# A searched program order without warm-up matmuls, and the last output stores on two queues

## Chip, cores, metric

One core of a Trainium2 chip. The metric is the device time of that core in microseconds, from the first instruction to the last. All outputs are right.

## The reference

Attention with a mask made by clusters, then two large matrix products with an exact gelu between them. Cut to what matters:

```python
# q, k, v: 4 x 8 x 768 x 64   centroids: 8 x 16 x 64   (32 "heads" of 768 x 64)
q_assign = argmax(einsum('bhsd,hcd->bhsc', q_n, c_n))      # nearest of 16 centroids
k_assign = argmax(einsum('bhsd,hcd->bhsc', k_n, c_n))
mask     = q_assign[..., :, None] == k_assign[..., None, :]
scores   = where(mask, q @ k.T / 8, -1e9)
x        = softmax(scores) @ v                             # then 3072 x 512
out      = gelu(x @ w_in) @ w_out                          # w_in 512 x 2048, w_out 2048 x 512
```

## The kernel before

The kernel does not leave the order of its instructions to a scheduler. A long string, `TABLE`, names every operation once, and `Plan.run` emits them in that order. The order on each engine and the moment at which a buffer comes free both follow from it. A word such as `evq0@DVE` puts an operation on another engine than its usual one. A word `warm256` is no work at all: a matmul on a constant tile into a spare PSUM bank, there to keep TensorE busy.

```python
TABLE = (
    "cent loadq0 loadq1 zero3 loadk1 dm loadk0 hiq0 zero2 ident ssq ones hik0 exptab root "
    "eps loq0 warm256 warm256 ... (18 in all) trq0 rnorm lok0 hiq1 loadk2 cn chi "
    "warm256 warm256 trk0 clo loq1 evk0 warm256 warm256 ctr evq0@DVE hik1 lok1@DVE cc "
    "warm256 ... (7) asnk0 asnq0 amax0 ge0 ... warm256 warm256 ohtr0 ... "
    # ... some 2,000 more words ...
    "fc2_3_P4_2_1 c122_3 stc1223 c212_3 stc2123 "
)

class Plan:
    def run(self, table):
        # ... cut ...
        for word in table:
            name, _, eng = word.partition("@")
            if name.startswith("warm"):
                self.filler(int(name[4:]))
                continue
            op = by_name[name]
            assert op not in done and done.issuperset(op.deps), name
            # ... takes its buffers, which have to be free ...
            op.emit(*([eng or op.eng] if op.alt else []))

plan = Plan(POOLS, lambda n: nc.tensor.matmul(warm_ps[:, 0:n], dm[:, 0:128],
                                              dm[:, 128:128 + n], start=True, stop=True))
```

Words that the argument needs, for head i:

- `loadq`, `loadk`, `loadv`: the head's inputs come in. `hi` casts q or k to 16 bits, `lo` subtracts to get the rest ("split"); most run on GpSimd.
- `trq`, `trk`, then `evq`, `evk`: six transposes on TensorE and the copy out of PSUM (heads 0 to 9). Later heads are transposed by a DMA (`dtr`).
- `asn`: small matmuls with 16 columns against the centroids; `amax` and `ge` turn them into a one-hot tile; `ohtr` (TensorE) or `ohd` (DMA) transposes it; `putk`, `putq` write it into the 16 spare rows of the transposed k and q. A score matmul then adds a large constant where the clusters agree.
- `sc`, `exp`, `av`, `rec`, `norm`: scores, exponentials (ScalarE), attention times V, normalisation. `fc1`, `gelu`, `fc2`: the two products, the second by a seven-product (Strassen) scheme whose sums (`S`, `t`, `ws`, `c`, `u`, `p`) VectorE, GpSimd and ScalarE share. `st`: output stores.

The one-hot write, and the store:

```python
def put_q(eng="DVE", i=i, e=e):                      # 16 x 768, SBUF to SBUF (PSUM for heads 0-7)
    src = T["ohps", i0][64 * e:64 * e + C, :]
    dst = T["qT", i][D:D + C, :]
    # ... ScalarE's form cut ...
    nc.vector.tensor_scalar(dst, src, float(VAL), None, op0=ALU.mult)

def store(name, j, t, col, due):
    st = add("SP", 0.36, due, lambda: nc.sync.dma_start(
        out=out_w[b][:, NJ * t + j, col * DB:(col + 1) * DB],
        in_=T[name, b, j]), [sums_out[name, j]], dma=0.45, name=f"st{name}{j}{b}")
```

The softmax here doesn't subtract the row's maximum and nothing guards it: scores larger than these inputs give would overflow.

## Time and profile before

| | before |
|---|---|
| time | 291.55 us median of 3 runs (291.4 to 291.79) |
| span of the profiled execution | 289.8 us |
| TensorE busy | 284.4 us, 3398 matmuls, of which 32 warm-ups |
| first score matmul in the chain | 11.27 us |
| first first-layer matmul in the chain | 44.76 us |
| last matmul ends | 286.62 us |
| last matmul to the end | 3.18 us |

The last four rows are read from the chain of work that ended last. A chain line gives start, duration, engine, tile written, source line and how many instructions stand in a row. They cut the span in four parts: the start, the middle stage (attention of the first heads), the long stretch of products mixed with later heads, and the tail. The prediction below shows these lines.

### The profile page before, as it was taken

How to read it: one execution, taken by the hardware profiler on the slowest of the kernel's cores; microseconds unless marked ns; L12 is line 12 of the kernel's file. 1: busy time of each engine (PE TensorE's matmuls, PEld its weight loads, DVE VectorE, ACT ScalarE, POOL GpSimd, SP SyncE). 2: the span in 40 equal slices, each digit the busy share in tenths (PEclk: the TensorE clock that was granted, in tenths of full speed). 3: DMA queues.
4: the chain of work that ended last, by engine and by line, in shares of the span. 5: the costliest groups of instructions: out<-in, count | busy, mean ns of one | idle time of the engine just before them, and what ended most of it. 6: DMA issues, size and time to landing. Idle time of an engine off the chain costs nothing.

```text
span 289.8 us, 8355 instructions
## 1 busy us (share of the span) xinstructions
PE 284.4 (98%) x3398; PEld 213.0 (73%) x3398; DVE 204.2 (70%) x494; ACT 235.1 (81%) x333; POOL 108.0 (37%) x148
## 2 busy tenths in 40 slices
PE   8999999999999999999999999999999999999995
PEld 6887766677677777765677878766687788756884
DVE  4989788397998778643489875725778833787863
ACT  4899988699799999977799988957699988599510
POOL 5898834609120631117202031605622271328000
PEclk9999999999999999999999999999999999999999
DMA  7999998899666799976479899753134213200023
GB/s 249 249 268 248 256 214 230 207 174 177 160 175 139 146 227 187 188 192 168 127 156 177 156 222 187 191 128 75 27 30 118 56 50 97 77 2 0 20 74 127
DMA packets 78038, 43.11 MB, mean 149 GB/s; under 512 B 55472, under 2 KB 78000, under 8 KB 78000
## 3 DMA queue, kind: packets, MB, share of 16 engines
q1 hardware_dynamic: 73488, 38.16, 57.7%
q0 software_dynamic: 4224, 4.19, 8.9%
q8 instruction: 26, 0.43, 0.6%
q10 hardware_dynamic: 288, 0.23, 0.3%
q14 instruction: 12, 0.10, 0.1%
HBM read 27.30 MB, written 6.29 MB: 116 GB/s over the span
## 4 chain that ended last, share of the span: by engine, by line
PE 96%; DVE 2%; ACT 1%; issue 0%; DVEq 0%
PE op L1233 25%; PE hp L918 22%; PE sc_ps L783 21%; PE x_ps L815 12%; PE fx_ps L1054 6%; PE asn_ps L615 2%; PE warm_ps L372 2%; PE tr_ps L573 2%; DVE kqT L714 1%; DVE kqT L723 1%; PE asn_ps L613 1%; PE asn_ps L612 1%; PE oh_ps L691 1%; ACT p_sb L792 1%; PE fin_ps L886 0%
## 5 line engine op out<-in xcount | busy, mean ns | idle before, releaser
L792 ACT ACTIVATE p_sb<-sc_ps 128x768 f16<-128x768 f32 x192 | 146.0, 810 | 9.7 <-PE sc_ps L783 6.8
L783 PE MATMUL sc_ps<-kqT 80*128 80x384 f16 x384 | 93.5, 325 | 0.6 <-DVE kqT L714 0.3
L918 PE MATMUL hp<-xt,w_in_sb 128*128 128x384 f16 x384 | 65.6, 326 | 0.0
L815 PEld LDWEIGHTS <-p_sb 128*128 128x128 f16 x1152 | 47.2, 97 | 10.4 <-DVE x_tok L842 0.6
L1233 PEld LDWEIGHTS <-g 128*128 128x128 f16 x480 | 45.3, 97 | 12.6 <-DVE g L948 0.2
L931 ACT ACTIVATE g<-hp 128x768 f16<-128x768 f32 x48 | 38.9, 810 | 19.0 <-PE hp L918 18.5
L918 PEld LDWEIGHTS <-w_in_sb 128*128 128x128 f16 x384 | 36.4, 98 | 22.9 <-issue 0.2
L815 PE MATMUL x_ps<-vaug,p_sb 128*128 128x65 f16 x1152 | 51.6, 193 | 0.0
L1233 PE MATMUL op<-w_out_sb,g 128*128 128x256 f16 x288 | 40.9, 272 | 0.0
L783 PEld LDWEIGHTS <-kqT 80*128 80x128 f16 x384 | 31.6, 98 | 4.7 <-DVE kqT L714 0.5
L1233 PE MATMUL op<-w_st,g 128*128 128x256 f16 x192 | 27.3, 272 | 0.0
L518 POOL TENSOR_TENSOR st<-k_raw,st 128x384 f16<-128x384 f32 x18 | 17.0, 943 | 24.9 <-DVE st L382 18.4
L518 POOL TENSOR_TENSOR st<-q_raw,st 128x384 f16<-128x384 f32 x21 | 19.8, 947 | 13.4 <-ACT st L380 8.6
L382 POOL CAST st<-q_raw 128x384 f16<-128x384 f32 x16 | 8.4, 531 | 40.9 <-DMA q_raw<-in_q_dram 24.9
L631 DVE TENSOR_REDUCE asb<-asn_ps 128x192 f32<-128x384 f32 x24 | 13.2, 551 | 14.8 <-PE asn_ps L615 14.6
L382 POOL CAST st<-k_raw 128x384 f16<-128x384 f32 x16 | 8.6, 537 | 35.4 <-DMA kqT<-st 16.3
L1233 PEld LDWEIGHTS <-S 128*128 128x128 f16 x192 | 18.0, 97 | 5.0
L842 DVE TENSOR_TENSOR x_tok<-x_ps,rec 128x384 f16<-128x384 f32 (+1 forms) x40 | 19.0, 476 | 1.1
L835 DVE RECIPROCAL rec<-x_ps 128x6 f32<-128x6 f32 (+1 forms) x40 | 7.4, 186 | 11.7 <-PE x_ps L815 10.7
L615 PEld LDWEIGHTS <-kqT 128*128 128x128 f16 x288 | 12.0, 96 | 3.4
L1233 PE MATMUL op<-w_st,S 128*128 128x256 f16 x96 | 13.9, 272 | 0.0
L1233 PE MATMUL op<-w_out_sb,S 128*128 128x256 f16 x96 | 13.8, 272 | 0.0
(125 smaller groups left out, 405.6 us busy)
## 6 DMA issues: line engine op xcount, KB each, us to landing
q_raw<-in_q_dram SPq DMA_DIRECT2D x32, 192.0 KB, 3.5
v_raw<-in_v_dram SPq DMA_DIRECT2D x32, 192.0 KB, 3.5
out_dram<-c SPq DMA_DIRECT2D x48, 128.0 KB, 2.0
k_raw<-in_k_dram SPq DMA_DIRECT2D x31, 192.0 KB, 3.4
w_in_sb<-in_moe_w_in_dram POOLq DMA_DIRECT2D x4, 512.0 KB, 10.4
w_out_sb<-in_moe_w_out_dram POOLq DMA_DIRECT2D x4, 512.0 KB, 8.6
kqT<-st SPq DMA_TRANSPOSE x22, 4.3
k_raw<-in_k_dram ACTq DMA_DIRECT2D x1, 192.0 KB, 3.2
```

The source lines that it names most:

```text
L382: engine[eng].tensor_copy(o, i)
L518: engine[eng].tensor_sub(t[:, :, D:2 * D], T[w + "raw", i], t[:, :, 0:D])
L615: nc.tensor.matmul(o, t[:, js], c_cat[:, h].rearrange("p a c -> p (a c)"), start=True, stop=True)
L631: nc.vector.tensor_reduce(out=T["asb", i], in_=T["asn", i].rearrange("p n w (a c) -> p n w c a", a=2), axis=AX.X, op=ALU.add)
L783: nc.tensor.matmul(s_ps[:, e, 0:QB], T["kT", i][0:D + C, c * 128:(c + 1) * 128], T["qT", i][0:D + C, t * QB:(t + 1) * QB], start=True, sto ...
L792: nc.scalar.activation(T["p", i, t][:, 2 * cp:2 * cp + 2, :], T["sc", i, t, cp][:, :, 0:QB], ACT_FN.Exp, bias=0.0, scale=float(scale))
L815: nc.tensor.matmul(o, T["p", i, t][:, ch, jj * 128:(jj + 1) * 128], vaugs[turn("va", i)][:, ch, 0:D + 1], start=(ch == 0), stop=(ch == N - 1))
L842: nc.vector.tensor_tensor(T["xtok", b][:, h // 2, j0:j0 + nn, h % 2 * D:(h % 2 + 1) * D], T["x", key][:, :, 0:D], T["rec", key].to_broadca ...
L918: nc.tensor.matmul(T["hp", hb, fp][:, e, 0:QB], w_in_sb[:, m, f * 128:(f + 1) * 128], T["xt", b][:, m, t * QB:(t + 1) * QB], start=(m == 0 ...
L931: nc.scalar.activation(T["g", hb][:, :, fp, :], T["hp", hb, fp][:, :, 0:QB], ACT_FN.Gelu, bias=0.0, scale=1.0)
L1054: nc.tensor.matmul(o, a[p](m), r[p](m), start=start and m == 0, stop=m == 1, skip_group_check=not start)
L1233: nc.tensor.matmul(T["op", b, key], a()[:, f, j * 128:(j + 1) * 128], w[:, f, :], start=(start and f == 0), stop=(f == NB - 1), skip_group ...
```

## The change

The intent: put the stores of the last row tile on two queues, so that one does not wait for the issue of the other; and take a new order from a search on a model that charges VectorE for the one-hot writes' drains and assumes that the clock rises later. That search left out all 32 warm-ups.

```diff
-    "cent loadq0 loadq1 zero3 loadk1 dm loadk0 hiq0 zero2 ident ssq ones hik0 exptab root "
-    "eps loq0 warm256 warm256 warm256 ... trq0 rnorm lok0 hiq1 loadk2 cn chi warm256 warm256 trk0 ...
+    "cent loadq1 ones dm zero3 loadk0 exptab ssq loadq0 zero2 root eps rnorm cn hik0 hiq0
+     lok0 chi clo loq0 loadk1 ident trk0 evk0 ctr trq0 hik1 cc lok1 hiq1 evq0@DVE ...
 ... (the 2,037 remaining words stand in a new order; the tail of it:)
-    "... c122_3 stc1223 c212_3 stc2123 "
+    "... stc2213 fc2_3_P3_2_0 c222_3@DVE stc2113 stc2223@ACT fc2_3_P3_2_1 c122_3
+     fc2_3_P4_2_0 fc2_3_P4_2_1 c212_3 stc2123 stc1213 stc1223@ACT "
 ...
-            st = add("SP", 0.36, due, lambda: nc.sync.dma_start(
+            st = add("SP", 0.36, due, lambda eng: engine[eng].dma_start(
                 out=out_w[b][:, NJ * t + j, col * DB:(col + 1) * DB],
-                in_=T[name, b, j]), [sums_out[name, j]], dma=0.45, name=f"st{name}{j}{b}")
+                in_=T[name, b, j]), [sums_out[name, j]], dma=0.45, name=f"st{name}{j}{b}",
+                alt={"SP": 0.36, "ACT": 0.36} if b == B - 1 and j == 2 else {"SP": 0.36})
```

By engine, the new order also moves ten two-input operations, net, from VectorE to GpSimd (245 to 235 on VectorE, 73 to 83 on GpSimd). Eight of them are subtractions of q or k (`lo`, 128x384).

## The prediction

> **What bounds the kernel now.** I read the busy table first, then the stretches by engine, then the chain that ended last, once for the first 46 us and once for the last 24 us.
>
> The page's busy and slice parts:
>
> ```profile
> PE 284.4 (98%) x3398; PEld 213.0 (73%) x3398; DVE 204.2 (70%) x494; ACT 235.1 (81%) x333; POOL 108.0 (37%) x148
> ...
> DMA  7999998899666799976479899753134213200023
> ```
>
> TensorE is counted busy for 98% of the span. That number alone would also be written by an engine that waits, because the matmuls overlap (a pair of score matmuls shows 0.49 us in the timeline and is 0.33 us apart in the chain). So I count the work from the chain instead. It gives these paces: 8 first-layer matmuls in 1.30 us (0.1625 each), 4 score matmuls in 0.65 (0.1625), 18 attention-times-V in 0.55 (0.0306), 156 second-layer in 17.04 (0.109), 96 of the last batch's first layer in 15.74 (0.164), small assignment matmuls about 0.025, transposes 0.34 per six (0.057). With the counts of the program: 384 x 0.1625 = 62.4; 384 x 0.1625 = 62.4; 1152 x 0.0306 = 35.2; 672 x 0.109 = 73.4; 112 x 0.164 = 18.4; 480 x 0.025 = 12.0; 182 x 0.057 = 10.3. Sum 274.1 us of useful TensorE work, the same in both kernels.
>
> The chain in order of time, of the early and the late part:
>
> ```profile
> 1.36 4.02 PE warm_ps L372 x18
> 5.38 0.64 PE tr_ps L573 x6
> ...
> 7.02 0.22 PE warm_ps L372 x2
> ...
> 7.35 0.77 PE warm_ps L372 x7
> 8.70 0.74 PE trs_ps L573 x12
> ...
> 11.27 0.38 PE sc_ps L783 x2
> ...
> 44.76 1.30 PE hp L918 x8
> ```
>
> ```profile
> 269.58 17.04 PE op L1233 x156
> 286.62 0.02 issue
> 286.65 0.42 DVE c L1279
> ```
>
> TensorE's part of the run goes from 1.36 to 286.62, 285.3 us. Less 274.1, 11.2 us are not useful work. Warm-up matmuls on constants take 4.02 + 0.43 + 0.22 + 0.77 + 0.22 + 0.12 = 5.8 of them. About 0.5 is the first two groups of transposes at a slower pace (0.64 and 0.58 for six, later 0.34). 4.9 us remain as gaps. Up to the first score matmul (11.27) the useful work is 3.35 us. Between the first score and the first first-layer matmul (11.27 to 44.76, 33.5 us) it is 34.04 - 3.35 = 30.7, so 2.8 us of gaps lie there. From 44.76 to 286.62 (241.9 us) there is 239.9 of work, so gaps of under 2.
>
> The stretches show what else is full in the middle stage:
>
> ```profile
> core 0: us, PE busy (x) PEld busy (x) DVE busy (x) ACT busy (x) POOL busy (x), PEclk, DMA share, GB/s
> ...
> 15.00:20.00 5.00, 5.00 (x104) 4.20 (x101) 4.31 (x12) 4.79 (x8) 4.82 (x8) 1.00 1.12 271
> 20.00:25.00 5.00, 4.80 (x98) 3.89 (x95) 4.57 (x12) 4.65 (x8) 4.99 (x9) 1.00 1.18 261
> ...
> 35.00:40.00 5.00, 4.63 (x81) 3.51 (x80) 4.29 (x11) 4.33 (x7) 1.71 (x4) 1.00 1.07 191
> ```
>
> VectorE is at 4.3 to 4.6 of 5 us, ScalarE at 4.3 to 4.8, and the DMA engines are at their full share. No single engine is the bound from 15 to 45 us; four are nearly full together. After 50 us TensorE alone is.
>
> **What the Trainium skill says.** (1) "Trainium Kernel Development and Optimization", section "Performance Expectations", calls matmul busy time a bad metric because matmuls are pipelined; the trace agrees (98% busy, 11 us without useful work), which is why I used the chain. (2) "TensorE: Matmul & The Clock Gate", Part 1, says that the array starts at half clock and goes to full clock after some 3.4 us of sustained activity, in a window that runs freely. The trace agrees: the first 18 warm-up matmuls take 4.02/18 = 223 ns each, those at 7.02 take 110 ns. The change of pace falls between 6.45 and 7.02, some 5.5 us after the first matmul. The PEclk row is 1.00 throughout and doesn't show it; only the pace does. (3) The same page, Part 4, says that transposes do not count as busy in the same way for this gate. No stretch of the trace here is only transposes, so the trace can't say. (4) "Trainium Kernel Development and Optimization", "Key Constraints": DMAs issued from several engines share the same 16 DMA engines, and issuing from several only saves the sequencer's issue time. Here an output store takes 332 ns to issue and 1.7 to 2.2 us to land.
>
> **The change part by part.**
>
> Warm-ups: all 32 are gone from the new order, 18 ahead of the first transpose, 13 before the first score, one right before it. None stands between useful work after 11.3 us, so their removal frees at most what lies on the prefix chain: 0.22 (before the one-hot transpose), 0.12, and up to 0.25 of the 0.77 group, which ended after the evacuation it covered for. About 0.5 us gained, if nothing else changed.
>
> But they also raised the clock. The new kernel's first matmul waits for a transpose's input, about 5.5 us. I walk the new prefix with durations from the old timeline. Both kernels issue the same four loads, but the new one puts head 1's q ahead of head 0's, and splits k first, which landed at 4.37. Cast 0.51, subtract 0.56: 5.5. Six transposes at half clock 0.64: 6.2. VectorE does the centroid cast (0.82), a subtract (0.23) and the q subtract (0.56) first, so the evacuation starts at 7.0; the old one started at 7.06. q's transposes end at about 7.75, and the assignment matmuls of head 0 start at 7.8 (old: about 8.1). If TensorE is still cold they take 1.2 us instead of 0.57, the twelve transposes of head 1 1.28 instead of 0.74, the one-hot transposes 0.64 instead of 0.45, six more 0.64 instead of 0.44, and head 1's assignments 1.2 instead of 0.57: 2.2 us more in all. With the old spacing (5.5 us from activity to full clock) the clock would rise at about 11, so most of this is paid, less the 0.5 gained and the 0.3 of the earlier start. I put the first score 1.2 us later (0.5 to 2), at about 12.5, and 0.6 us more lost on cold scores after it (0 to 2).
>
> Middle stage: the useful TensorE work up to the first-layer start is 34.4 instead of 34.0, ScalarE has 40 exponentials instead of 39. What moves is off VectorE: two subtractions fewer there, three more on GpSimd, one evacuation to ScalarE. VectorE's work falls from about 29.2 to 28.2 us (counts times durations of this trace: one-hot writes 0.55 + gap, evacuations 0.47, subtractions 0.46). And the new order spreads the four one-hot writes that now stand in one row (19.63 to 21.95), behind which a transpose waits. The search saw these drains, so I expect it to take 1.7 of the 2.8 us of gaps. GpSimd gets 16 subtractions of 0.945, 12 casts and 8 V casts: about 25.6 us plus some 5 of weight DMA issue, of 33. That fits, barely.
>
> Later: the same TensorE work, some other order. Of the 1.9 us of gaps I give it 0.9.
>
> Tail: two stores of the last row tile go to ScalarE's queue. In the old order SyncE's last issues are at 285.86, 286.29 and 287.10; the last follows VectorE's last add (286.65 + 0.42), so nothing was queued in front of it and a second queue has nothing to save. Worse, in the new SyncE order a store of row tile 1, whose data is ready long before, stands behind the very last one. It is issued 0.33 us later and should end the run: +0.3.
>
> Sum: +1.2 + 0.6 - 1.7 - 0.9 + 0.3 = -0.5 us, so 291.0.
>
> **Rivals.** *The clock rises as early as before* (the activity of transposes and assignments from 5.5 us is enough, and the window falls well): then the prefix costs nothing, the first score comes at 10.9 or so, and the sum is about 288.5 to 289. For it: the pieces stand close from 7 us on. Against it: gaps between 6.2 and 7.1, and matmuls of 16 columns that leave the array mostly idle. *The clock rises only when the scores flow* (transposes don't count): cold until 16 to 18 us, everything in between at half pace, 2 us more than in my sum: 293 to 295. For it: the skill's Part 4. Against: nothing in this trace. *The new DMA order becomes the wait*: the new order issues 26 head loads and all eight weight loads before the first layer instead of 22 and seven, 4 x 0.19 + 0.5 = 1.3 MB more at some 250 GB/s, 5 us of a DMA stage that is already full. Where these stand ahead of a load that is needed at once, it costs 1 to 3 us; where they are only early, nothing. *A gain of over 2%* would need 5.8 us: all gaps (4.9) and no cold loss. The floor is 5.5 + 274.1 + 3.2 = 282.8 in the trace, and the stage with four full engines makes it out of reach.
>
> **Range and chances.** The terms are small and of both signs; the cold clock (+0 to +4 together) is the widest, the middle stage (0 to -2.4) the next. A range of 288.3 to 294.3 us should hold it eight times in ten. Over 2% faster (below 285.7) 0.03, over 2% slower (above 297.4) 0.04, the rest within.
>
> **What would show it.** The first score matmul later than 11.27 by about 1 us, with transposes at 107 ns each up to 10 us or later, confirms the cold prefix; at 57 ns it refutes it. From the first score to the first first-layer matmul less than 33 us confirms the middle stage. The last SyncE issue should be a store that waits for nothing but its turn, 0.33 us after the one before; a span that ends as soon after the last matmul as before (3.2 us) refutes that. It is all wrong if GpSimd or a head load holds up the transposes between 12 and 45 us.

## The result

| | median | range |
|---|---|---|
| before (4 runs) | 291.67 us | 291.4 to 291.98 |
| after (4 runs) | 292.83 us | 292.39 to 293.24 |

The ratio is 1.0039, with a 95% interval of 1.0021 to 1.0057. Here and below a ratio is the mean time of one kernel's runs over the mean of the other's runs in the same rounds, so it is not quite the ratio of the medians quoted. The change made the kernel 0.4% slower: within 2%, inside the predicted range, but on the other side of zero from the predicted -0.5 us. Busy time of the kernel after:

```profile
PE 279.7 (96%) x3366; PEld 209.7 (72%) x3366; DVE 202.6 (70%) x483; ACT 237.5 (82%) x331; POOL 120.8 (42%) x161
```

TensorE lost its 32 warm-ups and is busy 4.7 us less, yet the span is 1.3 us longer. GpSimd is busy 12.8 us more. The chain of the kernel after, early and late part:

```profile
6.01 0.82 PE tr_ps L569 x6
...
8.83 1.25 PE trs_ps L569 x12
...
10.54 0.44 PE tr_ps L569 x6
11.57 0.48 PE sc_ps L779 x2
...
44.40 1.35 PE hp L914 x8
...
270.33 17.04 PE op L1230 x156
287.38 0.02 issue
```

TensorE now stands idle until 6.01 us. The twelve transposes at 8.83 take 1.25 us, 104 ns each; the six at 10.54 take 0.44, 73 ns each, with the clock now up. The first score comes 0.30 us later than before (11.57 against 11.27), the first first-layer matmul 0.36 us earlier (44.40 against 44.76), the last matmul ends 0.76 later (287.38 against 286.62), and the span 1.3 later. The final 156 matmuls take 17.04 us in both, so nothing is slower once the last product runs. By parts:

| part | before | after | difference |
|---|---|---|---|
| start of span to first score | 11.27 | 11.57 | +0.30 |
| first score to first layer | 33.49 | 32.83 | -0.66 |
| first layer to last matmul's end | 241.86 | 242.98 | +1.12 |
| last matmul to the end | 3.18 | 3.72 | +0.54 |
| span | 289.8 | 291.1 | +1.3 |

The new order has also moved 0.32 us more useful TensorE work ahead of the first layer (counts of matmuls by the paces given in the prediction). So in this pair of profiles the middle stage gained 1.0 us of gaps, and the long stretch, with 0.32 us less to do, lost 1.4. (Other executions of the same order lost less in the long stretch; see below the table of the experiments.) I looked for those 1.4 us by the starts of all matmuls in the two traces, taking as a gap what exceeds the normal pace by more than 0.12 us: 0.88 us in all before, 2.82 us after. The largest of the kernel after: 0.32 us at 62.8, 0.49 at 114.2, 0.42 at 116.4, 0.27 at 216.8 and 0.45 at 234.8. The wait view names the releasers; its columns are waiter, releaser, total idle us, count, longest:

```profile
PE tr_ps L569 <- DVE st L514: 6.0, 1, 6.0
...
PE sc_ps L779 <- DVE kqT L719: 0.3, 1, 0.3
PE op L1230 <- DVE p L378: 0.3, 1, 0.3
```

The second line is the stall at 234.8: a score matmul waits for a one-hot write. The timeline of the kernel after around it (start, duration, engine, line, operation, operands, count, and in brackets idle time before and its releaser):

```profile
232.63 0.42 DVE L944 TENSOR_TENSOR wf<-wf,w_in_sb 128x512 f16<-128x512 f16 x1
233.08 1.58 DVE L719 TENSOR_SCALAR kqT<-ohT 16x768 f16<-16x768 f16 x2
233.13 1.32 POOL L944 TENSOR_TENSOR wf<-w_in_sb,wf 128x512 f16<-128x512 f16 x1 [2.31 <-DVE wf L944]
...
234.81 0.48 PE L779 MATMUL sc_ps<-kqT 80*128 80x384 f16 x2 [0.29 <-DVE kqT L719]
```

Two one-hot writes, which take 0.35 us each elsewhere, take 1.58 us together. In that time GpSimd does a weight sum (233.13 to 234.45, `ws4_1`): the second write ends 0.21 us after it. (The bracket gives 0.29 us of idle time where my gap is 0.45: it counts from the modelled end of the matmul before, I count from starts.) All one-hot writes out of the DMA-made tile, by line, in the kernel before and then after (count: median/mean/longest ns):

```profile
L714 DVE TENSOR_SCALAR kqT<-ohT x23: 350/355/766, 61.9 to 225.7; 16x768 f16<-16x768 f16 x23
L723 DVE TENSOR_SCALAR kqT<-ohT x21: 350/352/949, 58.5 to 230.7; 16x768 f16<-16x768 f16 x21
```

```profile
L719 DVE TENSOR_SCALAR kqT<-ohT x21: 350/352/1195, 55.6 to 233.5; 16x768 f16<-16x768 f16 x21
L710 DVE TENSOR_SCALAR kqT<-ohT x19: 351/355/1028, 55.2 to 231.1; 16x768 f16<-16x768 f16 x19
```

The medians agree, but the longest went from 0.95 to 1.20 us. I checked this against GpSimd's instructions, over thirteen profiles (all but that of new_early_old_late). All 424 writes that start while no GpSimd instruction runs take 350 to 356 ns. Of those that start while one runs, 87 last as long as it still has to run, plus 209 to 222 ns (mean 215); the other 21 start with 172 ns of it left or less and take 351 to 389. The Trainium skill, page "SBUF — State Buffer", section "Who interferes with whom", says that VectorE and GpSimd share a port pair under an exclusive lock, so that whichever issues first holds it for its whole instruction and the other blocks; copies, casts and one-input scalar operations in a two-port mode are among those that take it. The trace agrees, with the numbers just given. Long writes number 6 of 44 before, 2.3 us over the 350 ns in all, and 9 of 40 after, 4.7 us over. Of the nine long writes after, five met a q or k subtraction, as against one of six before; no large gap of TensorE follows those five. The two meetings that a TensorE wait follows (62.8 and 234.8) were with weight sums. The one at 62.8 (`t2_2`) is new on GpSimd. The one at 234.8 is not: `ws4_1` ran on GpSimd before, too, and there it stretched a one-hot write at 229.34 to 0.91 us, with no gap of TensorE behind it. What is new there is its place in the order.

The stalls at 114.2 and 116.4 have another cause. VectorE's and TensorE's timeline of the kernel after:

```profile
112.04 0.35 DVE L719 TENSOR_SCALAR kqT<-ohT 16x768 f16<-16x768 f16 x1 [1.25 <-DMA ohT<-oh]
...
114.22 0.72 PE L811 MATMUL x_ps<-vaug,p_sb 128*128 128x65 f16 x18 [0.32 <-DVE x_tok L838]
...
115.16 0.36 DVE L378 CAST st<-k_raw 128x384 f16<-128x384 f32 x1 [1.00 <-DMA kqT<-st]
...
116.39 0.60 PE L1230 MATMUL op<-w_out_sb,g 128*128 128x256 f16 x4 [0.25 <-DVE p L378]
```

Here VectorE waits 1.25 us for a DMA transpose ahead of a one-hot write and 1.00 us for a staging buffer that a DMA transpose still reads. What TensorE needs next (a normalisation, a copy out of PSUM) stands behind these in VectorE's row. The chain of the kernel after shows what stands ahead of the second wait:

```profile
98.58 3.72 DMA kqT<-st
...
103.82 5.18 DMA q_raw<-in_q_dram
...
109.93 5.21 DMA kqT<-st
115.16 0.36 DVE st L378
```

A head's q load that took 5.18 us to land came first, and the transpose that needs it then took 5.21 us. So the stall at 116.4 goes back to a late head load as well as to a late transpose.

The tail, in SyncE's timeline, before and then after:

```profile
287.10 0.33 SPq L1213 DMA_DIRECT2D out_dram<-c  x1
```

```profile
287.85 0.81 SPq L1209 DMA_DIRECT2D out_dram<-c  x2
```

Before, the last store alone is issued after the last sum. After, a second store follows it (`stc1213`, of an earlier row tile, whose data had long been ready), and the pair takes 0.81 us to issue against 0.33: 0.48 us more.

### The profile page after: what moved, and what is told of

Same layout as the page of the kernel before. It is cut to its first block, busy times and chain, and to the rows that moved or that the text cites. A ratio compares the mean times of both kernels' runs of the same rounds, so it can differ in the third digit from the quotient of the medians.

```text
span 291.1 us, 8286 instructions
## 1 busy us (share of the span) xinstructions
PE 279.7 (96%) x3366; PEld 209.7 (72%) x3366; DVE 202.6 (70%) x483; ACT 237.5 (82%) x331; POOL 120.8 (42%) x161
## 4 chain that ended last, share of the span: by engine, by line
PE 86%; DMA 6%; DVE 3%; ACT 2%; POOL 1%; issue 1%; SPq 0%; ACTq 0%
PE op L1230 23%; PE hp L914 22%; PE sc_ps L779 18%; PE x_ps L811 9%; PE fx_ps L1050 6%; DMA kqT<-st 3%; ACT p_sb L788 2%; PE asn_ps L611 2%; PE tr_ps L569 2%; DMA q_raw<-in_q_dram 2%; DMA k_raw<-in_k_dram 1%; PE asn_ps L608 1%; PE asn_ps L609 1%; DVE kqT L719 1%; PE fin_ps L882 1%
## 5 line engine op out<-in xcount | busy, mean ns | idle before, releaser
L1230 PEld LDWEIGHTS <-g 128*128 128x128 f16 x480 | 45.6, 97 | 12.8 <-issue 0.5
L1230 PE MATMUL op<-w_out_sb,g 128*128 128x256 f16 x288 | 40.3, 272 | 0.3 <-DVE p L378 0.3
L514 POOL TENSOR_TENSOR st<-k_raw,st 128x384 f16<-128x384 f32 x24 | 22.8, 956 | 23.7 <-DVE st L378 21.0
L514 POOL TENSOR_TENSOR st<-q_raw,st 128x384 f16<-128x384 f32 x23 | 21.6, 941 | 9.4 <-ACT st L376 6.7
L378 POOL CAST vaug<-v_raw 128x384 f16<-128x384 f32 x20 | 10.7, 540 | 28.7 <-PE x_ps L811 17.5
L378 POOL CAST st<-q_raw 128x384 f16<-128x384 f32 x15 | 7.7, 512 | 27.7 <-DMA q_raw<-in_q_dram 16.3
L569 PE MATMUL tr_ps<-ident,st 128*128 128x128 f16 x108 | 9.6, 229 | 6.0 <-DVE st L514 6.0
L378 DVE COPY p<-op 128x256 f32<-128x256 f32 x19 | 8.0, 422 | 10.0 <-PE op L1230 9.8
L569 PEld LDWEIGHTS <-st 128*128 128x128 f16 x120 | 8.5, 106 | 7.7 <-DVE st L514 6.0
```

The costliest lines, as they stand in the source:

```text
L378: engine[eng].tensor_copy(o, i)
L514: engine[eng].tensor_sub(t[:, :, D:2 * D], T[w + "raw", i], t[:, :, 0:D])
L569: nc.tensor.transpose(t_ps[:, j * 128:(j + 1) * 128], T[w + "st", i][:, j, :], ident)
L1230: nc.tensor.matmul(T["op", b, key], a()[:, f, j * 128:(j + 1) * 128], w[:, f, :], start=(start and f == 0), stop=(f == NB - 1), skip_group ...
```

## The experiments

My theory after reading the two traces: leaving out the warm-ups costs 1 us or more; the middle stage really gained; the store order costs 0.5 us; the lost time of the long stretch is VectorE held up by GpSimd sums and by DMA transposes. The rival: the warm-ups do not matter at all (in the pair of profiles the first score is only 0.3 us later), and the new late order is simply worse.

One quantity has to be watched in every profile here: when the trace's record of the granted clock shows the step from half to full. The page's clock row shows full clock for all the time ahead of the trace's first record, so it does not show a cold start.

| kernel | clock full at | first score | first layer | last matmul ends | to the end |
|---|---|---|---|---|---|
| before | 6.8 | 11.15 | 44.6 | 286.61 | 3.21 |
| after | 9.9 | 11.55 | 44.3 | 287.36 | 3.72 |
| tail_on_before | 4.1 | 11.11 | 44.57 | 286.58 | 3.70 |
| tail_mended | 11.6 | 12.10 | 44.95 | 287.02 | 3.23 |
| warm_back | 6.8 | 10.79 | 43.56 | 286.23 | 3.70 |
| no_warm_before | 15.0 | 12.62 | 47.43 | 290.27 | 3.21 |
| warm_tail | 6.0 | 10.55 | 43.44 | 285.72 | 3.22 |
| collisions_out | 6.7 | 10.84 | 43.59 | 285.65 | 3.22 |
| after_again | 13.8 | 12.36 | 46.48 | 288.53 | 3.70 |
| warm_filled | 4.5 | 11.11 | 43.86 | 285.78 | 3.72 |
| best_a | 5.3, half at 8.7, full at 12.1 | 12.94 | 45.68 | 287.61 | 3.21 |
| best_b | 6.4 | 10.70 | 43.45 | 285.38 | 3.21 |

The times in this table are starts of matmuls in the traces; they differ by up to 0.2 us from the chain's lines, which begin a line where the matmul's wait ended. The stretch from the first layer to the last matmul's end (the column "last matmul ends" less "first layer") varies with the execution: 242.01 us before, and with the new order 243.06 (after), 242.67 (warm_back), 242.28 (warm_tail), 242.05 (after_again, the same program as after) and 242.07 (tail_mended, the same up to the last stores). So the +1.12 of the first pair is the largest draw of the new order, and in two executions nearly nothing was lost there (0.4 us with the 0.32 us of work that left this stretch). The old order also has a bad draw: 242.84 in no_warm_before. The two splices below are left out of it. The experiments ran in three sets, each with the kernel before in between: the first four below (its median there 291.51 us), the next four (291.89), both on one chip, and the last four on another (291.60).

### tail_on_before: the tail alone

```diff
 (kernel before, with the new store())
-    ... stc1213 ... stc2223 ... c122_3 stc1223 c212_3 stc2123
+    ... stc2223@ACT ... c122_3 c212_3 stc2123 stc1213 stc1223@ACT
```

> The kernel before, all of it but the last stores: row tile 2's c22 and c12 go to ScalarE's queue, and row tile 1's c12 store stands on SyncE behind the very last store. If the tail is a cost of the new order by itself (my reading), the last SyncE issue stands 0.33 us after the one before, the time from the last matmul to the end grows from 3.18 us to about 3.7, and the kernel is 0.3 to 0.6 us slower than before (about 292.1). If the rival holds (the end is set by the landing of any of the last stores, and the tail of the new kernel is longer only because of chance), it is within 0.15 us of before.

Measured: 292.10 us (291.78 to 292.92), ratio to before 1.0019 (1.0003 to 1.0034). SyncE's last line in its timeline:

```profile
287.07 0.81 SPq L1213 DMA_DIRECT2D out_dram<-c  x2
```

All else in this kernel is the kernel before, its first layer starts within 0.03 us of it, and the tail has grown from 3.21 to 3.70 us. So the two-queue tail, with its order of stores, costs 0.5 us by the profile, and the timed runs agree (0.19% is 0.55 us).

### tail_mended: the kernel after, the early store put back ahead

```diff
-    ... c212_3 stc2123 stc1213 stc1223@ACT
+    ... c212_3 stc1213 stc2123 stc1223@ACT
```

> The changed kernel with one store moved: row tile 1's c12 store goes ahead of the last store on SyncE, the two stores on ScalarE's queue stay. My reading: last matmul to end falls from 3.72 to about 3.2 us, and the time by 0.3 to 0.6 us against the changed kernel (292.83 to about 292.3). Two queues are then worth nothing against one: the tail is as long as before, not shorter. Rival: the two queues do save something once the order is mended, then the tail is under 3.0 us.

Measured: 292.64 us (291.89 to 293.48), ratio 1.0036 (1.0017 to 1.0055). The tail in its profile:

```profile
287.50 0.33 SPq L1209 DMA_DIRECT2D out_dram<-c  x1
```

The profile shows the tail back at 3.23 us, so the order of the two stores is the whole of the 0.5 us, and the second queue saves nothing (3.21 us before, with one). In time the gain does not show against the kernel after (1.0036 beside 1.0039 in the first runs): the clock rose at 11.6 us in the profiled execution, and the runs spread over 1.6 us. This is a miss for a timed effect of 0.5 us, and the reason to make the start repeatable first.

### warm_back: the kernel after with warm-ups

```diff
-    ... ident trk0 ...
+    ... ident warm256 (19 times) trk0 ...
```

> The changed kernel with 19 warm-up matmuls again ahead of its first transpose. By the clock theory the transposes of heads 0 and 1 fall from 0.64 to 0.66 us for six, and 1.25 for twelve, to 0.35 and 0.74, and the first score comes 0.5 to 1.0 us sooner (10.6 to 11.1 instead of 11.57); whether the end moves as much depends on the later stalls: 0.3 to 0.9 us off the changed kernel. Rival: the prefix is set by the arrival of the first k and by VectorE, not by TensorE's clock; then the first score moves by under 0.2 us.

Measured: 291.35 us (291.02 to 291.71), ratio to before 0.9989 (0.9974 to 1.0004). Chain:

```profile
10.81 0.48 PE sc_ps L781 x2
...
43.67 1.35 PE hp L916 x8
```

These 19 matmuls fill time in which TensorE waited anyway. The clock is full at 6.8 us, the first score 0.76 us and the first layer 0.73 us earlier than in the kernel after, and the time goes from 1.0039 of before to 0.9989: 0.5% or 1.5 us. That is more than the expected 0.3 to 0.9, and more than the 0.73 us that the profiles show up to the first layer; another 0.4 us of their difference lies after it (242.67 against 243.06), where executions differ anyway. From the first score to the first layer it takes 32.86 us, as the kernel after does (32.83) and 0.6 less than before, so the middle stage's gain is the order's own, not one of the clock.

### no_warm_before: the kernel before without warm-ups

```diff
-    ... all 32 words warm256
```

> The kernel before without its 32 warm-up matmuls and nothing else changed. By the clock theory its first transposes run at 107 ns each until about 4 us after the first one, the first score comes 0.3 to 1.0 us later than 11.27, and the kernel is 0.2 to 1.0 us slower than before. Rival: the warm-ups stand in the way of real work as much as they help; then it is within 0.2 us of before, or faster.

Measured: 294.46 us (293.74 to 295.29), ratio 1.0097 (1.0077 to 1.0117), 2.8 us slower. Chain:

```profile
12.77 0.65 PE sc_ps L780 x2
14.06 0.64 PE sc_ps L780 x2
...
47.59 1.30 PE hp L915 x8
```

In this execution a pair of score matmuls takes 0.65 us where others have about 0.33 by start-to-start distance: the clock is still at half and rises at 15.0 us. The expectation, 0.2 to 1.0 us, was far too small. By the table, 1.5 of the 3.7 us in this profile, of the slowest of its six runs, come before the first score, 1.35 between it and the first layer, and 0.8 after, where no warm-up ever stood. The rival that the warm-ups do not matter is out, in both orders. In the same profile the 16-column assignment matmuls start 0.026 us apart while cold (8.53 to 9.12 us in its timeline) and 0.026 us apart later; in the kernel after 0.025 when warm. They do not slow with the clock. Transposes do: 107 ns each cold, 57 warm.

### warm_tail: warm-ups and the mended tail

```diff
 (warm_back)
-    ... c212_3 stc2123 stc1213 stc1223@ACT
+    ... c212_3 stc1213 stc2123 stc1223@ACT
```

> The changed kernel with both mends: 19 warm-up matmuls ahead of its first transpose, and row tile 1's store ahead of the last one. If the two costs are separate, as I think, they add: warm_back's 291.35 less the 0.5 us of the tail, about 290.8, 0.7 us faster than before; tail 3.2 us. If the late stalls only move when the phase moves, it is within 0.3 us of before.

Measured: 291.57 us, ratio 1.0006 (0.9975 to 1.0036). Its runs are 290.72, 293.72, 292.86, 290.75, 291.28 and 291.85: they spread over 3.0 us, where warm_back's lay within 0.7. The profiled execution has the tail of 3.22 us and ends its matmuls at 285.72, the best so far. The lowest runs fit the expectation and the middle does not. The spread is looked at under best_a below.

### collisions_out: the GpSimd sums moved from the one-hot writes

```diff
 (warm_tail)
-    ... exp7b1 t1_2 t2_2@POOL sc7b0 ... putq9 fev021 ...
+    ... exp7b1 t1_2 sc7b0 ... putq9 t2_2@POOL fev021 ...
-    ... c210_2 ws2_1 dfin31 ... norm28_1 fc2_2_P6_1_1 ...
+    ... c210_2 dfin31 ... norm28_1 ws2_1 fc2_2_P6_1_1 ...
```

> warm_tail with two weight sums moved: one VectorE sum behind the one-hot writes at 233 us, so that the GpSimd sum which waits for it no longer runs during them, and one GpSimd sum at 61 us behind the one-hot write there. My reading: a one-hot write waits for the GpSimd instruction that is running when it starts and takes 0.35 us otherwise; then those two writes fall from 0.96 and 1.20 us to 0.35, the stalls of 0.33 us (at 62 us) and 0.45 us (at 234 us) of the changed kernel go, and the kernel is 0.4 to 0.8 us faster than warm_tail. Rival: TensorE waits there for something else that comes just as late; then the writes get short and the time stays within 0.2 us of warm_tail.

Measured: 290.92 us (290.10 to 291.96), ratio 0.9968 (0.9948 to 0.9988). The second place in its timeline:

```profile
231.41 0.73 DVE L721 TENSOR_SCALAR kqT<-ohT 16x768 f16<-16x768 f16 x2
...
233.09 0.48 PE L781 MATMUL sc_ps<-kqT 80*128 80x384 f16 x2
```

The pair of writes that took 1.58 us takes 0.73, and the score matmul after it waits for nothing: the stall of 0.45 us is gone. So at this place the GpSimd sum was the cause, and moving it removed it. The first place did not change: a write of 1.22 us at 61.8 and a stall of 0.41 at 64.4 are still there. GpSimd had nothing else in its queue, and ran the moved sum just as early; a later place in the table does not mean a later start. The 0.65 us between the medians of warm_tail and this kernel is of the size of the stall but below warm_tail's spread, so the timeline carries this verdict, not the times. In the two profiled executions the span hardly moved (288.94 and 288.86 us): a gap of 0.43 us at 116.9 stands in this one, where warm_tail's has 0.27 and 0.15 near 115 and 117.

### new_early_old_late and old_early_new_late: splicing the orders

```diff
 new_early_old_late: the order after up to the first fc1 (with 19 warm256), then the rest
                     in the order before; 17 words (eight loads and what needs them)
                     deferred until a buffer is free
 old_early_new_late: the order before up to the first fc1, then the rest in the order after,
                     with the mended tail; 4 loads deferred
```

> The changed order with warm-ups up to the first first-layer matmul, the order of before from there to the end, tail of before included. If the new order gains in its early stage and loses late, this is the best of all: 1.2 to 1.8 us faster than before (289.7 to 290.3). Rival: the late stalls of the changed kernel are set by how early it runs ahead of its loads; then they come here too, and it is within 0.7 us of before.

> The order of before with its warm-ups up to the first first-layer matmul, the changed order from there on, with the mended tail. By my reading, first-layer start at 44.7 us as before and then the stalls of the changed kernel at 62, 216 and 234 us, perhaps 114 and 116: 0.5 to 1.4 us slower than before. Rival (early part to blame for the late stalls): within 0.3 us of before.

Measured: 315.10 us, ratio 1.0805, and 294.68 us, ratio 1.0098. The first says nothing on the question, as its longest wait of TensorE shows:

```profile
PE x_ps L814 <- ACT vaug L379: 7.1, 1, 7.1
```

TensorE waits 7.1 us for the cast of a V tile; loads of V were among the deferred words. The splice itself made the wait. In the same profile the granted clock fell to half three times (50.9 to 54.3, 85.1 to 95.3 and 105.5 to 112.4 us), which adds to the loss. In the second, the first layer starts at 45.96 us, 1.36 later than before (TensorE waits 0.9 us for an exponential), and 1.57 us at 61 us are a wait ahead of an assignment matmul for a DMA transpose, where the order of before has none. From first layer to last matmul it takes 243.23 us, 1.2 longer than before, and this wait is more than the whole of it. Without it the stretch would be 0.3 us shorter than before, or the same when the 0.32 us of work that stands ahead of the first layer is counted, though stalls of 0.32 at 66 and 0.45 at 236.6 are there. So the second splice doesn't show that the late order loses time by itself. Two orders that each hold buffers across the cut cannot be swapped at it.

### after_again: the kernel after, unchanged

> The changed kernel unchanged, on the same chip as the three that follow, with more runs. Expected 292.4 to 293.3 us with a spread of some 1.5 us, because without warm-ups the moment at which TensorE's clock rises moves from run to run; before spreads less.

Measured: 293.46 us (292.67 to 294.82), ratio 1.0065 (1.0044 to 1.0086). Chain:

```profile
12.50 0.65 PE sc_ps L779 x2
...
46.58 1.36 PE hp L914 x8
```

The same program had its clock full at 9.9 us in the first profile and at 13.8 in this one, and here its first scores are cold: 0.65 us a pair, the first layer 2.18 us later. The start of the kernel after is a matter of luck, and the pair of profiles that I read first held a good draw: a first score 0.3 us late, where this one is 1.2 late. The median lies just above the expected range, and the spread of 2.2 us is wider than the expected 1.5; before spread over 1.1. In this execution the stalls at 114 and 116 do not appear: between 110 and 119 us VectorE does not wait for a DMA. Nor does it in tail_mended, where the first layer is 0.65 us later than in the kernel after. So they differ between executions; that the phase of the loads decides is likely, but was not tested by itself.

### warm_filled: warm-ups also in the later holes

```diff
 (kernel after, as in warm_back, and)
-    ... trq0 hik1 ... evk1 ohtr0 ... loadk4 sc0a2 ...
+    ... trq0 warm256 x3 hik1 ... evk1 warm256 x2 ohtr0 ... loadk4 warm256 sc0a2 ...
```

> The changed kernel with 25 warm-ups: 19 ahead of the first transpose, 3 behind head 0's q transposes, 2 ahead of the first one-hot transposes, 1 ahead of the first score. By the clock theory 1.2 to 1.8 us faster than the changed kernel in the same rounds (291.0 to 291.6), as with the 19 alone. Rival (the warm-ups in the gaps delay real work): no faster than 292.

Measured: 291.30 us (291.09 to 292.38), ratio 0.9993 (0.9978 to 1.0009). Beside after_again on the same chip (1.0065) the warm-ups are worth 0.72%, 2.1 us; beside the first pair they were worth 1.5. The six extra ones after the first transpose gave nothing over warm_back's 0.9989.

### best_a and best_b: what the experiments point to

```diff
 best_a: warm_filled with the mended tail, ws2_1 behind norm28_1, t1_2 and t2_2@POOL behind putq9
 best_b: best_a and
-    ... dfin10 ... exp15b1 ohd16 dtr18 ... exp15b0 hik22@DVE putq17 ... norm15_1 sc16a1
+    ... ohd16 dfin10 ... exp15b1 dtr18 ... exp15b0 putq17 ... norm15_1 hik22@DVE sc16a1
```

> The changed kernel with the 25 warm-ups, the mended tail, and both weight-sum moves, the one at 61 us now with the VectorE sum that releases it, so that it can't run during the one-hot write. Expected: the stalls at 62 us (0.33 to 0.41) and 234 us (0.45) both gone, tail 3.2 us, 290.0 to 290.6 us: 1.2 to 1.8 us faster than before, and with less spread than the run with the collisions taken out. Rival: a one-hot write near 62 us collides with the next GpSimd instruction, and 0.4 us of it stays.

> As the run before it, and VectorE no longer stands behind two DMA transposes near 112 us: the one-hot transpose of head pair 16 is issued ahead of an output transpose, and one cast that waits for a free staging buffer stands behind the next normalisation. If the stalls of the changed kernel at 114 and 116 us (0.49 and 0.42) come from VectorE standing in line behind those transposes, none is left there, and the time is 0 to 0.5 us under the run before it, depending on whether they showed there. Rival: moving them only moves the wait.

Measured: best_a 291.19 us (290.31 to 292.64), ratio 0.9992 (0.9966 to 1.0017). best_b 290.47 us (290.23 to 291.69), ratio 0.9966 (0.9950 to 0.9981). The expectation for best_a (290.0 to 290.6, less spread than collisions_out) was missed: its runs spread over 2.3 us against 1.9, and near 64 us the wait stayed (see best_b). The stall at 234 us is gone in both.

The profiled execution of best_a is one where the clock rose at 5.3 us, fell back to half at 8.7 and rose again at 12.1, in steps of 3.41 us. TensorE's timeline, and the stretches from 5 to 10 and 10 to 15 us (columns as in the prediction's stretches), of best_a:

```profile
7.62 0.51 PE L572 MATMUL tr_ps<-ident,st 128*128 128x128 f16 x6 [0.96 <-DVE st L517]
...
9.12 1.44 PE L572 MATMUL trs_ps<-ident,st 128*128 128x128 f16 x12
```

```profile
5.00:10.00 5.00, 3.47 (x53) 2.82 (x52) 4.72 (x13) 3.27 (x8) 2.96 (x4) 0.87 0.89 301
10.00:15.00 5.00, 5.00 (x66) 3.69 (x64) 3.50 (x9) 3.37 (x6) 3.60 (x6) 0.79 0.94 237
```

The six transposes at 7.62 take 0.51 us, at full clock. The twelve at 9.12 take 1.44, at half. Here the granted clock shows in the page's own numbers: 0.87 and 0.79. TensorE was busy 3.47 us of the first stretch, and 1.92 of the 3.41 us between the rise and the fall, with waits of at most about 1 us, and mostly with transposes and 16-column matmuls. A clock that was up did not stay up. Each run's mean granted clock says more: half a clock for 3.41 of 290.8 us takes 0.006 off the mean, and this run (292.60 us) has 0.994. Of best_a's other runs, the one of 292.64 has 0.994, too, and the other four (290.31 to 291.44) have 0.998 or more. In collisions_out the two slowest runs (291.44 and 291.96) have 0.994, and warm_tail's slowest (293.72) has 0.986. So a clock that falls again explains most of these spreads; warm_tail's 292.86, at 0.998, it does not.

best_b, whose clock rose at 6.4 and stayed, ends its matmuls at 285.38. Its stall near 64 us remains:

```profile
62.54 1.15 POOL L947 TENSOR_TENSOR w_st<-w_out_sb 128x512 f16<-128x512 f16 x1 [1.18 <-DVE w_out_sb L947]
62.65 1.33 DVE L947 TENSOR_TENSOR w_st<-w_out_sb 128x512 f16<-128x512 f16 x1
64.11 0.36 DVE L841 TENSOR_TENSOR x_tok<-x_ps,rec 128x192 f16<-128x192 f32 x1
```

Once the one-hot write was out of the way, a VectorE sum with two SBUF inputs met GpSimd's sum instead: 1.33 us against 0.42 elsewhere, with the normalisation behind it. TensorE still loses 0.65 us there (0.64 in best_a); the wait moved. The gaps at 114 and 116 are absent in the profiles of both best_a and best_b, so the two extra moves of best_b are not shown to have cured them. best_b is 0.7 us under best_a by the medians, more than the 0 to 0.5 expected, but best_a's two runs with the lower clock are in that. It has the lowest ratio, 0.3% faster than the kernel before with an interval that excludes 1; collisions_out (0.9968) is not told apart from it.

## Why the prediction was right, and where its parts were not

The median of 292.83 us lies in the range, 1.8 us above the predicted 291.0. Against the kernel before, -0.5 us was predicted and +1.3 came in the spans, so the sign of the small difference was wrong. The errors of the parts partly cancel, so that the number lies so near is in part luck.

- **The cold start (predicted +1.2 and +0.6).** The mechanism held: transposes at 107 ns each past 8 us, and warm-ups that were worth more as clock than they cost as time. The size is a draw. The pair of profiles read first has +0.3 to the first score and no cold scores; after_again has +1.2 and cold scores. Putting warm-ups into the new order gained 1.5 and 2.1 us in two sets of runs, around the predicted 1.8. A step inside was wrong: the assignment matmuls were to take 1.2 us instead of 0.57 cold, twice. They keep 0.025 to 0.026 us, so 1.26 of the 2.2 us of cold cost had no ground. Against that, the first transposes were put at 5.5 us and came at 6.01 and 6.22. That after_again hits the +1.2 is therefore luck in the size. In the first profile the clock rose at 9.9, in the later ones of the same start (tail_mended, after_again) at 11.6 and 13.8, around the "about 11" of the prediction.
- **The first rival (clock as early as before) and the second (only when scores flow).** Neither is right for all executions. At 9.9 us in the kernel after no score had run, so scores are not needed; without warm-ups in the kernel before it took until 15.0, after the scores had begun.
- **The middle stage (predicted -1.7).** Right in sign. It gave -0.66 us in the chain, -1.0 with the useful work that moved into it counted; with warm-ups restored it gave the same 32.86 us. The reason given was wrong. The four one-hot writes were to be spread, but they stand in one row in the kernel after, too, from 20.03 to 22.33 us (19.63 to 21.95 before):

```profile
20.03 0.55 DVE L719 TENSOR_SCALAR kqT<-oh_ps 16x768 f16<-16x768 f16 x1
20.61 1.15 DVE L710 TENSOR_SCALAR kqT<-oh_ps 16x768 f16<-16x768 f16 x2
21.77 0.56 DVE L719 TENSOR_SCALAR kqT<-oh_ps 16x768 f16<-16x768 f16 x1
```

  TensorE's gap behind them (0.36 us at 22.0 before) is gone all the same, so the order around them changed; what closed the gaps was not tested. The prediction's VectorE share of 4.3 to 4.6 of 5 us holds for the lines that it shows; from 30 to 35 us it is 3.65, from 40 to 45 us 3.92.
- **Later (predicted -0.9).** This is the step that failed. I read it as "the same work in another order" and gave half the gaps away as a gain. (274.1 less 34.04 is 240.1, so the gaps were 1.8 us, not 1.9.) No execution of the kernel after shows the gain: the stretch took 1.12 us longer than before in the first profile (1.4 of gaps) and 0.04 longer in after_again. I charged GpSimd only for its own time in the middle stage, not VectorE for waiting while it runs. collisions_out shows this cause at one of the stalls (0.45 us); the one at 62.8 only turned into another wait of the same two engines. It is not the number of sums on GpSimd that did it, which fell, but where they run beside VectorE's writes. The stalls at 114 and 116 are DMA transposes that land late, in some executions only. The one of 0.27 at 216.8 stays open, and so does what the smaller gaps add up to.
- **The rival of the DMA order.** In the wait view no head load holds TensorE, and none did before the first layer. In the later part, where I had not looked, DMA transposes did, and one of them behind a q load of 5.18 us (the chain above). So this rival came true there in part, at one stall of 0.42 us in the first profile.
- **The tail (predicted +0.3).** The mechanism was exact: a store of an earlier row tile behind the last one. The term is mis-sized: two stores in a row take 0.81 us to issue where one alone takes 0.33, so 0.48 is added, and the tail grew by 0.54 (0.49 in tail_on_before).

## What to carry to other kernels

Price an instruction on GpSimd by what it does to VectorE at that moment, not only by its own length, and read the longest instance of a short VectorE operation beside its median. A filler matmul in time in which TensorE waits anyway brought the clock up earlier here (6.8 instead of 9.9 to 13.8 us) at no cost that showed, but did not always keep it up (best_a); leave it out only after several executions, since one profile may hold a lucky start. In the last microseconds put first into each queue what is ready first, and check a second queue by its last issue.

## What the Trainium skill lacked or had wrong

- "TensorE: Matmul & The Clock Gate", Part 1: the window of about 3.4 us agrees (steps of 3.41 us in best_a). It gives about half a microsecond of spread for the moment of the change, in matmuls issued back to back. One and the same kernel, sparse at its start, changed at 9.9 and at 13.8 us in two executions, 3.9 us apart.
- The same part has the clock fall after an idle window, and tells of a kernel whose clock swings because TensorE idles briefly and often, without saying how much idling it takes. In best_a it fell at 8.7 us, 3.4 us after it had risen, though TensorE was busy 1.92 of these 3.41 us and waited for no longer than about 1 us at a time.
- The same page, Part 4, says that transposes do not count as busy in the same way. In the kernel after, TensorE did nothing before 9.9 us but transposes and 16-column matmuls from 6.0 on, and the clock rose. Which of the two kinds counted, the runs do not separate.
- Part 1 has a floor of about 25 ns between the starts of narrow matmuls, measured at full clock. It does not say that the cold clock leaves them there: with 16 columns they start 0.026 us apart cold and 0.025 warm, while 128-column transposes go from 107 ns cold to 57 warm and a score pair from 0.65 to 0.33 us.
- "SBUF — State Buffer", "Who interferes with whom": the lock agrees. It does not say how long the wait outlasts the lock: the write ends 209 to 222 ns (mean 215, 87 cases) after the GpSimd instruction that it met. That a VectorE operation with two SBUF inputs contends with GpSimd is stated; best_b has its price, 1.33 us where others take 0.42.
